# Attention with a gated feed-forward block on one core: probabilities divided by their row sums before the transposes instead of outputs after them, the first pair in written order, the spatial weights split first

## The chip, the cores and the metric

The kernel runs on one core of a Trainium2 chip. The metric is the device time of one execution in microseconds (us); less is better. The time before is the median of three runs. PE is TensorE, DVE is VectorE, ACT is ScalarE, POOL is GpSimd, SP is SyncE, which issues the transfers; PEld is the weight load of TensorE.

## The reference

There are 8 batches, 8 heads, 576 positions and 64 numbers per head. First comes attention with a causal mask in blocks of 64 positions, then one gated feed-forward block over the heads put together (512 columns, 1024 inside), all in float32:

```python
def _attn_ref(q, k, v):
    scores = np.matmul(q, k.transpose(0, 1, 3, 2)) / np.sqrt(64)
    scores = np.where(block_i >= block_j, scores, -1000000000.0)   # blocks of 64
    scores = scores - np.max(scores, axis=-1, keepdims=True)
    attn = np.exp(scores)
    attn = attn / (np.sum(attn, axis=-1, keepdims=True) + 1e-09)
    return np.matmul(attn, v)

def _moe_ref(x, w_in, g_ln, w_sg, b_sg, w_out):       # x: (8, 576, 512)
    h = gelu_tanh(x @ w_in)
    u, v = h[..., :512], h[..., 512:]
    v_n = (v - mu) / np.sqrt(var + 1e-06) * g_ln
    v_s = np.einsum('ts,bsd->btd', w_sg, v_n) + b_sg[None, :, None]
    return x + (u * v_s) @ w_out
```

## The kernel before

**Numbers.** Operands of most matmuls are split into a high and a low part of a TensorE format (`q_h`, `q_l`, `xh`, `xl`, `wi_h`, `wi_l` and so on), and a product is three matmuls: high by high, low by high, high by low. A split is a copy into the high part on VectorE or ScalarE (the rows CAST) and a subtraction on GpSimd. The weights `w_in` and `w_out` come as 64-bit numbers and are put together from their words first (`from_f64`, L199: `Abs` with a scale on ScalarE, three operations on VectorE).

**Attention.** Two heads of one batch make a pair; the 32 pairs are the 32 slots of `slot` (L724). Rows of scores are tiled by five: tile 0 has 64 query rows, tiles 1 to 4 have 128, and tile i needs 64 + 128 i keys (64, 192, 320, 448, 576). For each tile and head, TensorE makes scores (`products`), VectorE adds the mask and finds the negative maximum while it copies them into the tile `prob` (`maximum`, L333, the row CUSTOM_DVE or ISA), and ScalarE takes the exponent in place and leaves the row sums in `sums` (`exponent`, L348). To multiply with `v`, TensorE transposes the probabilities in blocks of 128 columns into PSUM banks `pa`, `pb`, `pc`, `pd` (`turn0`, `turn2`, `turn1`, `turn_first`), ScalarE or VectorE copies the banks out (`pt`), and `av0`, `av2`, `av1` and `av00` add up the output, heads on partitions and positions along the row, in the bank `ob` and a corner of `pd`.

**The row sums.** `inverse` (L438), at the start of a slot, turns all ten sums per row into reciprocals `ri` on VectorE, and GpSimd spreads each over 64 columns (`rx`). `turn_sums` (L456) transposes `rx` in five matmuls into the bank `pe` and a corner of `pd`. `normalise` (L487) copies the output from PSUM to the tile `x` on ScalarE, multiplies it with `pe` and `pd` on VectorE and sends it to a spill buffer in DRAM. `split` (L497) makes `xh` and `xl` of it.

**A slot.** Slot n does the transposes and outputs of pair n and, between them, the scores of pair n + 1, in four steps: the first half of tile 4 and tile 1; the second half of tile 4; tiles 3 and 0; tile 2. Between these stand seven holes, `hole(g[0])` to `hole(g[6])`, each of which takes so many pieces of feed-forward work as the string of the slot says.

**Feed-forward work.** After the fourth pair of a batch, `begin` (L818) queues this batch's parts: five pieces of `v_part`, eight of `u_part`, eight of the batch before's `o_part`, eight of `s_part`. So slots 0 to 3 have no such work, slots 4 to 7 do that of the first batch, and so on; the last batch's stands behind slot 31. `v_part` puts into the queue `side` what other engines do next: the gelu, the moments, the centring and the scaling of the layer norm, which ends in the tiles `vh` and `vl` that `s_part` multiplies with the spatial weights `ws_h`, `ws_l`. `run_side` takes a few of these at set places of a slot. `o_part` (L674) reloads `x` from the spill buffer for the residual (`xr`), one column of 128 at a time, just before its matmuls; `x` and `xr` share a tag of three buffers.

The holes are set by strings, of which the first batch has its own, and the loading of weights by a share for each of the first nine slots:

```python
    WS = [2, 2, 2, 2, 4, 3, 4, 4, 3]
    PLAN = ["1111111", "1111111", "1111111", "1111112"]
    FIRST = ["1111111", "1111111", "1010101", "1010010"]
```

**Weights.** `weights` (L274) is a queue of loading steps: `w_in` for v, the gains `g_ln`, `w_in` for u in two halves, the spatial weights, `w_out`. `load_share(n, k)` takes steps in slot n by `WS`; `need(part)` takes all that are left of a part when the part begins.

**Order.** Only TensorE runs in the order in which the code is written (`PIN = "P"`, L58, L82). What the other engines do in which order, a scheduler decides when the kernel is built. PSUM has five banks for scores, `ob` and feed-forward sums, and three for the transposes, `pd` and `pe`. The first pair's scores are made ahead of slot 0 (L800 to L813), with four loading steps and the split of pair 1 between.

## Time and profile before

| | |
|---|---|
| median of 3 runs | 836.48 us (835.96 to 839.25) |
| profiled execution, its own time | 838.82 us |
| its span | 836.9 us |
| mean granted TensorE clock | 0.966 |
| busy: TensorE, VectorE, ScalarE, GpSimd | 94%, 64%, 51%, 42% |
| weight loads of TensorE, beside its matmuls | 78% |
| the chain that ended last | TensorE 63%, VectorE 20%, ScalarE 6%, transfers 5%, GpSimd 3%, issue 3% |
| DRAM | 45.78 MB read, 18.87 MB written, 77 GB/s over the span |

In the rows of a timeline the first number is the start in us from the span's start, the second the duration, then come engine, line, operation, result <- operands with buffer numbers left out, and the shape; `x4` stands for a run of four such instructions, and the duration is then that of the run. A bracket at the end holds the idle time of the engine just before, and what ended it. In rows of waits the three numbers are the idle time in all, the number of waits, and the longest. Matmuls stand under L86, transposes under L89, and what the other engines do under L99, since helpers record them; so it is the tile's name that tells a step. Two heads' tiles read alike.

Slot 0 begins near 24.4 us, slot 1 at 42.3, slot 2 at 52.9, slot 3 at 64.4, slot 4 at 75.1, slot 8 at 180.7. From there a batch of four slots takes near 97 to 101 us, and the last batch's feed-forward work fills 767.5 to the end.

### The profile page before, as it was taken

Reading aid. Unit: us, or ns where it says so; the run is one execution under the profiler, and the core shown is the slowest. Engines: PE = TensorE matmul, PEld = TensorE weight load, DVE = VectorE, ACT = ScalarE, POOL = GpSimd, SP = SyncE. Lnnn points to the kernel's source line nnn. Section 1 sums busy time; section 2 is a strip of 40 time slices with the busy share of each in tenths; the row PEclk is TensorE's granted clock in tenths of the full one; section 3 lists DMA queues with packets and bytes.
Section 4 is the critical chain, followed back from the end, with each engine's and each line's share of the span. In section 5 each row is a group of like instructions: output and inputs, shape, how many; then the busy total and the mean of one; then the engine's idle time right before and its main releaser. Section 6 shows DMA issues by size and latency. Waiting matters only on the chain.

```text
span 836.9 us, 15898 instructions
## 1 busy us (share of the span) xinstructions
PE 788.5 (94%) x5926; PEld 649.0 (78%) x5926; DVE 531.6 (64%) x1504; ACT 424.4 (51%) x1124; POOL 352.7 (42%) x402
## 2 busy tenths in 40 slices
PE   5798992999999999999999999999999999999998
PEld 3466871878878888887887878788787878878998
DVE  6876474894865658564776747766586647753432
ACT  4776663656654367344653357642764446531400
POOL 5445158461543417432372513634164323713251
PEclk8799995999999999999999999999999999999999
DMA  7233205221122112310133101321123201230031
GB/s 251 77 114 115 85 18 159 80 61 57 44 86 99 58 58 72 126 59 30 58 108 120 58 28 31 126 101 57 58 71 122 77 16 57 75 112 29 1 114 71
DMA packets 46912, 65.67 MB, mean 78 GB/s; under 512 B 4082, under 2 KB 22514, under 8 KB 46836
## 3 DMA queue, kind: packets, MB, share of 16 engines
q1 hardware_dynamic: 46836, 64.67, 24.1%
q8 instruction: 46, 0.75, 0.4%
q14 instruction: 30, 0.25, 0.1%
HBM read 45.78 MB, written 18.87 MB: 77 GB/s over the span
## 4 chain that ended last, share of the span: by engine, by line
PE 63%; DVE 20%; ACT 6%; DMA 5%; POOL 3%; issue 3%; SPq 0%; DVEq 0%; ACTq 0%; POOLq 0%
PE accs L86 14%; PE accv L86 13%; PE acco L86 9%; PE ob L86 9%; PE s L86 7%; PE pb L89 3%; DVE prob L99 3%; DVE bs L99 3%; DVE vh L99 2%; DVE vv L99 2%; PE pa L89 2%; PE accu L86 2%; ACT prob L99 2%; PE pc L89 2%; DMA xr<-spill 2%
## 5 line engine op out<-in xcount | busy, mean ns | idle before, releaser
L99 ACT ACTIVATE prob<-prob,negm 128x448 f32<-128x448 f32 (+3 forms) x320 | 178.0, 558 | 157.8 <-DVE negm L99 154.1
L99 DVE CUSTOM_DVE_ANT_0 prob<-s,mask 128x288 f32<-128x288 f32 (+2 forms) x320 | 119.4, 421 | 37.2 <-PE s L86 36.5
L99 POOL TENSOR_TENSOR q_l<-q_f,q_h 128x576 fp32r<-128x576 f32 x31 | 44.2, 1425 | 196.1 <-PE s L86 158.3
L86 PE MATMUL ob<-pt,v_f 128*64 128x512 f32 (+4 forms) x640 | 115.3, 452 | 0.0
L99 POOL TENSOR_TENSOR gl<-u,gh 128x288 fp32r<-128x288 f32 x64 | 52.3, 824 | 105.1 <-DVE gh L99 72.9
L86 PE MATMUL accs<-ws_h,vh 128*128 128x288 f32 x256 | 79.8, 312 | 8.9 <-DVE vh L99 8.9
L86 PE MATMUL s<-k_h,q_h 64*128 64x288 f32 (+1 forms) x372 | 86.7, 351 | 1.2 <-DVE negm L99 1.2
L86 PE MATMUL accs<-ws_h,vl 128*128 128x288 f32 x256 | 76.8, 300 | 6.1 <-POOL vl L99 6.1
L86 PE MATMUL accu<-xh,wi_h 128*128 128x288 f32 x256 | 78.6, 307 | 1.3 <-ACT wi_h L99 1.3
L86 PE MATMUL acco<-gh,wo_h 128*128 128x288 f32 x256 | 79.8, 312 | 0.0
L86 PE MATMUL acco<-gl,wo_h 128*128 128x288 f32 x256 | 76.5, 299 | 0.0
L86 PE MATMUL acco<-gh,wo_l 128*128 128x288 f32 x256 | 76.4, 299 | 0.0
L86 PE MATMUL accs<-ws_l,vh 128*128 128x288 f32 x256 | 76.2, 298 | 0.0
L86 PE MATMUL accu<-xh,wi_l 128*128 128x288 f32 x256 | 75.4, 295 | 0.3 <-POOL wi_l L99 0.3
L86 PE MATMUL accu<-xl,wi_h 128*128 128x288 f32 x256 | 75.6, 295 | 0.0
L86 PE MATMUL s<-k_l,q_h 64*128 64x288 f32 (+1 forms) x372 | 72.2, 298 | 0.0
L86 PEld LDWEIGHTS ob<-pt,v_f 128*64 128x64 f32 x640 | 40.1, 139 | 40.9 <-issue 20.8
L86 PE MATMUL accv<-wi_h,xh 128*128 128x512 f32 x160 | 66.2, 414 | 0.7 <-POOL xh L99 0.7
L99 DVE TENSOR_TENSOR xr<-acco,xr 128x288 f32<-128x288 f32 x64 | 29.0, 454 | 59.2 <-PE acco L86 21.7
L86 PE MATMUL s<-k_h,q_l 64*128 64x288 f32 (+1 forms) x372 | 66.1, 293 | 0.0
L99 DVE TENSOR_TENSOR u<-accs,u 128x288 f32<-128x288 f32 x64 | 28.7, 448 | 57.6 <-PE accs L86 57.6
L86 PEld LDWEIGHTS s<-k_h,q_h 64*128 64x128 f32 x372 | 49.6, 180 | 18.2 <-issue 12.4
(106 smaller groups left out, 2109.9 us busy)
## 6 DMA issues: line engine op xcount, KB each, us to landing
spill<-x SPq DMA_DIRECT2D x32, 288.0 KB, 3.0
xr<-spill SPq DMA_DIRECT2D x32, 288.0 KB, 3.1
out_T<-xr SPq DMA_DIRECT2D x32, 288.0 KB, 2.4
q_f<-in_qT SPq DMA_DIRECT2D x31, 288.0 KB, 3.1
k_f<-in_kT SPq DMA_DIRECT2D x31, 288.0 KB, 3.4
v_f<-in_v SPq DMA_DIRECT2D x32, 256.0 KB, 3.3
raw<-in_w_in SPq DMA_DIRECT2D x16, 256.0 KB, 5.0
raw<-in_w_out SPq DMA_DIRECT2D x8, 256.0 KB, 4.3
```

The lines of the kernel that those rows point to most:

```text
L86: return pin(nc.tensor.matmul(*a, **k), "P")
L89: return pin(nc.tensor.transpose(out, in_, identity), "P")
L99: return lambda *a, **k: pin(f(*a, **k), self.letter)
```

## The change

**The division moves ahead of the transposes.** `inverse`, `turn_sums` and the two products of `normalise` go; what is left of it, two copies and the spill, is called `leave`. Instead `Scores.divide` stands in three places behind the exponents, for tiles 4 and 1, 3 and 0, and 2: VectorE adds 1e-9 to the sums of those tiles and takes the reciprocals, and each probability tile is multiplied in place with its rows' reciprocals, tiles 4 and 3 on VectorE, 1 and 0 on GpSimd, 2 on ScalarE.

**Order and weights.** For the first pair, VectorE and ScalarE run in written order too, and its loading steps, three now, stand behind it. The spatial weights come second in the queue. `WS` and `FIRST` have other numbers. In `from_f64` the scaling moves from ScalarE to GpSimd.

**Spill and split.** `x` is split at the end of its own slot, except in the first two slots of a batch from the second batch on, whose splits wait until the end of the second one. `o_part` asks for `xr` one column ahead, and for the first column in the next batch's `u_part` (in the last batch, in `s_part`).

```diff
+    kept = set(PIN)
...
-        A.activation(m.bitcast(F32), hi.bitcast(F32), AF.Abs, scale=2.0**-112)
+        G.tensor_scalar(m.bitcast(F32), hi.bitcast(F32), 2.0**-112, None, op0=ALU.mult)
...
             ("v", load_gains()),
+            ("s", load_spatial()),
             ("u0", load_weight(w_in, slice(0, DH // 2), wi_h, wi_l)),
             ("u2", load_weight(w_in, slice(DH // 2, DH), wi_h, wi_l)),
-            ("s", load_spatial()),
...
+        def divide(self, *tiles):
+            i0, i1 = min(tiles), max(tiles)
+            ts = slice(i0, i1 + 1, max(i1 - i0, 1))
+            V.tensor_scalar_add(self.ri[:, ts, :], self.sm[:, ts, :], 1e-9)
+            V.reciprocal(self.ri[:, ts, :], self.ri[:, ts, :])
+            for i in tiles:
+                r, e = slice(0, QN[i]), EXT[i]
+                for a in (0, 1):
+                    x, c = self.prob[a][i][r, :e], self.ri[r, i, a : a + 1]
+                    if i == 2:
+                        A.mul(x, x, c)
+                    else:
+                        {4: V, 3: V, 1: G, 0: G}[i].tensor_scalar(x, x, c, None, op0=ALU.mult)
...
-        def normalise(self):
+        def leave(self):
             x = self.x = page(F32, S, "x")
             copy("a", x[:, BLK:], self.ob)
             copy("a", x[:, :BLK], self.o0)
-            V.tensor_tensor(x[:, BLK:], self.rp, x[:, BLK:], op=ALU.mult)
-            V.tensor_tensor(x[:, :BLK], self.t4[:, 128:192], x[:, :BLK], op=ALU.mult)
...
+        def reload(mo):
+            if mo < NC:
+                x_r[mo] = page(F32, S, "xr")
+                SP.dma_start(x_r[mo], spill.pop((b, mo)))
...
+            if fo == NC - 1 and b:
+                reloads[b - 1](0)
...
             if th == 0:
-                x_r[mo] = page(F32, S, "xr")
-                SP.dma_start(x_r[mo], spill.pop((b, mo)))
+                reload(mo + 1)
...
-    WS = [2, 2, 2, 2, 4, 3, 4, 4, 3]
+    WS = [2, 3, 3, 3, 8, 0, 3, 3, 2]
...
-    FIRST = ["1111111", "1111111", "1010101", "1010010"]
+    FIRST = ["1111111", "1111110", "0000011", "1111110"]
...
-        va.inverse()
         va.turn0(0)
...
             nx.exponents(4)
+            nx.divide(4, 1)
...
             nx.exponents(3, 0)
+            nx.divide(3, 0)
             nx.step4()
         va.av1()
         va.av00()
-        va.turn_sums()
         if nx:
             nx.exponents(2)
+            nx.divide(2)
         hole(g[4])
-        va.normalise()
...
+        va.leave()
+        wait = n // (H // 2) > 0 and n % (H // 2) < 2
+        pending.append(va.split)
+        if not wait:
+            while pending:
+                pending.popleft()()
...
+    kept.update("VA")
     sc = Scores(0)
     sc.step1()
     sc.exponents(1)
     sc.step2()
     sc.exponents(4)
-    weight_step()
+    sc.divide(4, 1)
     sc.step3()
     sc.exponents(3, 0)
-    split_qk(1)
-    weight_step()
+    sc.divide(3, 0)
     sc.step4()
     sc.exponents(2)
-    weight_step()
-    weight_step()
+    sc.divide(2)
+    split_qk(1)
+    for _ in range(3):
+        weight_step()
+    kept.difference_update("VA")
```

Three places show what the change moves. The first is VectorE at the start of the program; the rows ISA with `negm` are the maxima of the first pair, `w<-raw` and `w<-w` are pieces of `w_in`. Before:

```order
1 L99 CAST q_h<-q_f 128x576
2 L99 CAST k_h<-k_f 128x576
3 L99 TENSOR_SCALAR w<-raw 128x256
4 L99 SCALAR_TENSOR_TENSOR w<-raw,w 128x256
5 L99 TENSOR_SCALAR w<-raw 128x256
6 L99 SCALAR_TENSOR_TENSOR w<-w 128x256
7 L99 SCALAR_TENSOR_TENSOR w<-raw,w 128x256
8 L99 TENSOR_SCALAR w<-raw 128x256
9 L99 ISA prob_4_114,negm<-s,mask 128x288
```

After:

```order
9 L101 ISA prob_4_114,negm<-s,mask,negm 128x288
10 L101 ISA negm 128x1
11 L101 ISA prob_4_123,negm<-s,mask,negm 128x288
12 L101 ISA negm 128x1
13 L101 TENSOR_SCALAR ri<-sums 128x2x2
14 L101 RECIPROCAL ri<-ri 128x2x2
15 L101 TENSOR_SCALAR prob_4_114<-prob_4_114,ri 128x576
16 L101 TENSOR_SCALAR prob_4_123<-prob_4_123,ri 128x576
17 L101 ISA prob_3_112,negm<-s,mask 128x448
```

The weight pieces no longer stand ahead of the maxima; instead the division of tile 4, which needs ScalarE's exponents of tiles 4 and 1, stands ahead of the maxima of tile 3.

The second place is VectorE in slot 2, around the maxima of tile 2 of pair 3 (`prob_2_128` and `prob_2_137` are its two heads; `x<-pe,x` is the product with the transposed reciprocals). Before:

```order
L99 CAST q_h<-q_f 128x576
L99 ISA prob_2_128,negm<-s,mask 128x320
L99 ISA negm 128x1
L99 ISA prob_2_137,negm<-s,mask 128x320
L99 ISA negm 128x1
L99 CAST k_h<-k_f 128x576
L99 TENSOR_TENSOR x<-pe,x 128x512
L99 TENSOR_SCALAR ri<-sums 128x10
L99 TENSOR_TENSOR x<-pd,x 128x64
L99 RECIPROCAL ri<-ri 128x10
L99 CAST xh<-x 128x576
```

After:

```order
L101 TENSOR_SCALAR prob_4_132<-prob_4_132,ri 128x576
L101 TENSOR_SCALAR prob_4_141<-prob_4_141,ri 128x576
L101 ISA prob_2_137,negm<-s,mask 128x320
L101 ISA negm 128x1
L101 CAST k_h<-k_f 128x576
L101 TENSOR_SCALAR ri<-sums 128x2x2
L101 CAST xh<-x 128x576
L101 RECIPROCAL ri<-ri 128x2x2
L101 TENSOR_SCALAR ri<-sums 128x2
L101 TENSOR_SCALAR prob_3_130<-prob_3_130,ri 128x448
L101 TENSOR_SCALAR prob_3_139<-prob_3_139,ri 128x448
L101 RECIPROCAL ri<-ri 128x2
```

The products with `pe` and `pd` are gone, and two divisions of tile 3 stand between the sums of tile 2 and their reciprocal.

The third place is ScalarE in slot 9, the second slot of a full batch (`prob_2_110` and `prob_2_119` are tile 2 of the next pair, `u<-u` the gelu of u, ACT_TABLE_LOAD the change of function table). Before:

```order
L99 ACTIVATE prob_2_110,sums<-prob_2_110,negm 128x320
L99 COPY x<-ob 128x512
L99 COPY x<-pd 128x64
L99 ACTIVATE prob_2_119,sums<-prob_2_119,negm 128x320
L99 COPY u<-accu 128x288 x2
L99 ACT_TABLE_LOAD
L99 ACTIVATE u<-u 128x576 x4
L99 COPY pt<-pa 128x512
```

After:

```order
L101 ACTIVATE prob_2_110,sums<-prob_2_110,negm 128x320
L101 COPY x<-ob 128x512
L101 COPY x<-pd 128x64
L101 ACTIVATE prob_2_119,sums<-prob_2_119,negm 128x320
L101 COPY u<-accu 128x288
L101 ACTIVATE prob_2_110<-prob_2_110,ri 128x320
L101 ACTIVATE prob_2_119<-prob_2_119,ri 128x320
L101 COPY u<-accu 128x288
L101 ACT_TABLE_LOAD
L101 ACTIVATE u<-u 128x576 x4
L101 COPY pt<-pa 128x512
```

The two products of the division stand ahead of the last copy of u, the gelu of u and the copy of the bank `pa`.

More of the change, by code (lines that the diff above doesn't have):

```diff
@@ L80, in pbank @@
         return bank("p", name, 3)
+    kept = set(PIN)
     def pin(ins, e):
-        return tc.keep_in_program_order(ins) if e in PIN else ins
+        return tc.keep_in_program_order(ins) if e in kept else ins
     def mm(*a, **k):
@@ L305, in __init__ @@
             self.sm = sp.tile([P, NT, 2], F32, tag="sums", name="sums", bufs=3)
+            self.ri = sp.tile([P, NT, 2], F32, tag="ri", name="ri", bufs=2)
             G.memset(self.sm[:, 0, :], 1.0)
@@ L390, in __init__ @@
             self.v = vals.pop(n)
-            self.prob, self.sm = sc.prob, sc.sm
+            self.prob = sc.prob
             self.pt = {}
@@ L454, in turn_first @@
             copy("a", pt0[:BLK, :], t[:BLK, : 2 * BLK])
-        def turn_sums(self):
-            turn(self.t4[:, 128:256], self.rx[:, 0, :], ident)
-            t = self.rp = pbank("pe")
-            for i in range(1, NT):
-                turn(t[:, (i - 1) * P : i * P], self.rx[:, i, :], ident)
         def av(self, dst, j, pts, c0, n, start, stop):
@@ L522, in paced @@
     def paced(ins, e):
-        return ins if e in PIN else tc.keep_in_program_order(ins)
+        return ins if e in kept else tc.keep_in_program_order(ins)
     def gelu(tiles, after):
@@ L536, in accumulator @@
         return sbank(name)
+    reloads = {}
     def feed_forward(b):
@@ L542, in feed_forward, with v_part @@
         vn_t = sp.tile([P, DH], F32R, tag="vn_t", name="vn_t")
-        parts = (b, vv, vn, vn_t, u, g_s)
+        x_r = {}
+        def reload(mo):
+            if mo < NC:
+                x_r[mo] = page(F32, S, "xr")
+                SP.dma_start(x_r[mo], spill.pop((b, mo)))
+        parts = (b, vv, vn, vn_t, u, g_s, x_r, reload)
         return v_part(*parts), u_part(*parts), s_part(*parts), o_part(*parts)
-    def v_part(b, vv, vn, vn_t, u, g_s):
+    def v_part(b, vv, vn, vn_t, u, g_s, x_r, reload):
         need("v")
@@ L613, in v_part, with u_part @@
             side.append(("V", lambda st=st: scale(st)))
-    def u_part(b, vv, vn, vn_t, u, g_s):
+    def u_part(b, vv, vn, vn_t, u, g_s, x_r, reload):
         x_s = xs.pop(b)
@@ L641, in u_part, with s_part @@
                 yield "u"
-    def s_part(b, vv, vn, vn_t, u, g_s):
+    def s_part(b, vv, vn, vn_t, u, g_s, x_r, reload):
         need("s")
@@ L647, in s_part @@
             run_side(len(side))
+        reloads[b] = reload
         for dt in range(NC):
+            if dt == NC - 1 and b == B - 1:
+                reload(0)
             ghi, glo = page(F32R, S, "gh"), page(F32R, S, "gl")
@@ L672, in s_part, with o_part @@
                 yield "s"
-    def o_part(b, vv, vn, vn_t, u, g_s):
+    def o_part(b, vv, vn, vn_t, u, g_s, x_r, reload):
         need("o")
-        x_r = {}
+        if not x_r:
+            reload(0)
         for mo, th in [(mo, th) for mo in range(NC) for th in (0, 1)]:
@@ L768, in slot @@
         va.av00()
-        va.turn_sums()
         if nx:
             nx.exponents(2)
+            nx.divide(2)
         hole(g[4])
-        va.normalise()
-        last = n % (H // 2) == H // 2 - 1
-        if last:
-            for f in pending:
-                f()
-            pending.clear()
-            va.split()
+        va.leave()
[4 more added lines that the diff above has]
+                pending.popleft()()
         run_side(2)
@@ L788, in slot @@
         run_side(3)
-        for f in pending:
-            f()
-        pending.clear()
-        if not last:
-            pending.append(va.split)
+        if n % (H // 2) == 1:
+            while pending:
+                pending.popleft()()
         return nx
-    pending = []
+    pending = deque()
     last_o = []
```

9 lines of the change are left out of this document (removed).

## The prediction

> **What bounds the kernel now.** I read the page first, for the busy shares and the 40 slices, then a table of stretches cut where a slot begins, then the waits of TensorE, and last the timelines at the places where the table shows TensorE idle.
>
> ```profile
> span 836.9 us, 15898 instructions
> PE   5798992999999999999999999999999999999998
> 24.40:42.30 17.90, 15.27 (x97) 9.21 (x97) 15.66 (x53) 13.27 (x42) 9.61 (x12) 0.75 0.15 47
> 52.90:64.40 11.50, 10.37 (x96) 7.01 (x96) 8.91 (x33) 8.57 (x28) 5.39 (x7) 1.00 0.31 103
> 125.50:146.50 21.00, 6.03 (x24) 4.20 (x23) 8.62 (x9) 7.50 (x12) 18.07 (x18) 0.58 0.51 159
> 479.00:576.00 97.00, 95.89 (x742) 79.59 (x741) 63.99 (x180) 50.89 (x134) 40.71 (x44) 1.00 0.23 74
> ```
>
> In a row of the table the columns are length, TensorE, weight loads, VectorE, ScalarE and GpSimd busy, granted clock, DMA. Three kinds of time show. Four slots of one batch (479 to 576) are filled with matmuls: 95.89 of 97.00. The first slots have attention alone and are nearly full too (10.37 of 11.50), except slot 0, where VectorE has 15.66 of 17.90. And there is a hole of 15 us at 125 to 146, where the granted clock is 0.58. So most of the span goes by what TensorE executes; the opening and the hole go by what it waits for. The hole's waits and owners:
>
> ```profile
> PE accs L86 <- DVE vh L99: 8.9, 3, 5.8
> PE accs L86 <- POOL vl L99: 6.1, 3, 4.7
> 124.90 2.07 SPq L99 DMA_DIRECT2D w<-in_w_sgT  x4
> 134.76 4.63 POOL L99 TENSOR_TENSOR ws_l<-w,ws_h 128x576 fp32r<-128x576 f32 x3
> 136.07 2.06 DVE L99 TENSOR_TENSOR ws_l<-w,ws_l 1x576 fp32r<-1x576 f32 x1 [7.42 <-ACT ws_l L99]
> ```
>
> The spatial matmuls wait 8.9 + 6.1 = 15.0 us for the normalised tiles vh and vl; these stand on VectorE and GpSimd behind the splitting of the spatial weights, whose loads are issued only at 124.90.
>
> **Transposes that go.** Five rx transposes per pair:
>
> ```profile
> 51.56 0.33 PE L89 MATMUL pd<-ident,rx 128*128 128x128 f32 x1
> 52.16 0.38 PE L89 MATMUL pa<-ident,prob 128*128 128x128 f32 x2
> 498.49 0.33 PE L89 MATMUL pd<-ident,rx 128*128 128x128 f32 x1
> 499.01 0.47 PE L86 MATMUL accv<-wi_h,xh 128*128 128x512 f32 x1
> ```
>
> From the first of them to what follows, TensorE spends 0.60 us in the opening and 0.52 in a full slot. From slot 8 on there are 24 pairs, TensorE is full, and nothing else stands in that place: 24 x 0.52 = 12.5 us off (14.4 at 0.60). The pairs before are counted in the next two parts.
>
> **Slots 4 to 7, and the hole.** From the start of slot 4 to that of slot 8:
>
> ```profile
> 75.11 0.38 PE L89 MATMUL pa<-ident,prob 128*128 128x128 f32 x2
> 180.71 0.60 PE L89 MATMUL pa<-ident,prob 128*128 128x128 f32 x4
> 767.51 12.83 PE accv L86 x56
> 780.34 12.74 PE accu L86 x96
> 805.80 14.84 PE accs L86 x112
> ```
>
> That is 105.6 us. The last three rows, from the chain at the end where nothing else runs, price one batch's first three parts: 40.4 us. An attention slot has 10.37 busy less 0.60 for rx, 9.8, four are 39.2; so TensorE needs 79.6. With the spatial weights split in slot 0, what they held up is free. I do not expect 79.6: slot 6 gets no work in its first five holes, so it takes the length of a slot without work (worked out next, 14.8, where its content with two spatial pieces of 1.86 is 13.5: +1.3), the crossing from slot 5 to 6 gets the waits of the part after next (+4.4), and the layer norm still shares GpSimd with the output weights, whose scaling moves there (I allow 4). That makes 89.3, 16.3 off; ends 12 and 20.
>
> **The opening, slots 0 to 3.** Here the division lies open, for no feed-forward work fills the holes.
>
> ```profile
> 5.83 2.37 PE L86 MATMUL s<-w 64*128 64x288 f32 x14
> 12.28 0.45 DVE L99 CUSTOM_DVE_ANT_0 prob<-s,mask 128x288 f32<-128x288 f32 x1
> 24.40 1.56 PE L89 MATMUL pa<-ident,prob 128*128 128x128 f32 x6 [2.66 <-ACT prob L99]
> 50.45 0.46 DVE L99 CAST q_h<-q_f 128x576 fp32r<-128x576 f32 x1 [0.16 <-issue]
> 51.05 1.42 POOL L99 TENSOR_TENSOR q_l<-q_f,q_h 128x576 fp32r<-128x576 f32 x1 [5.35 <-DVE q_h L99]
> 51.65 1.13 DVE L99 CAST k_h<-k_f 128x576 fp32r<-128x576 f32 x1
> 52.65 0.19 ACT L99 ACTIVATION_READ_ACCUMULATOR prob<-prob,negm 128x1 f32 x1
> 52.90 0.44 PE L89 MATMUL pa<-ident,prob 128*128 128x128 f32 x2 [0.36 <-ACT prob L99]
> 53.68 0.20 ACT L99 ACTIVATION_READ_ACCUMULATOR prob<-prob,negm 128x1 f32 x1
> 54.10 0.66 PE L89 MATMUL pa<-ident,prob 128*128 128x128 f32 x4 [0.76 <-DVE x L99]
> 64.38 0.44 PE L89 MATMUL pa<-ident,prob 128*128 128x128 f32 x2 [0.37 <-ACT prob L99]
> ```
>
> The first pair: its maxima now start at 12.28, behind weight pieces. In written order they can start when the first scores are there, near 6.6, a part of the way into the row at 5.83. But VectorE then waits in turn for the exponents of tiles 4 and 1, and of 3 and 0, before the next maxima; adding up its 24 rows with these waits I come to 20.9 for the tile-2 transpose, where 24.40 stood: 3.5 off. Slot 0 then carries eight pieces of w_in, all of the spatial weights and the second pair's divisions through VectorE and GpSimd: between 0 and 9.5 longer than its 17.9 us; I take 5.
>
> Slots 1 to 3 repeat every 64.38 - 52.90 = 11.48 us. Tile 2 closes the loop. Before, head 0's transpose follows its exponent by 0.25 (52.65 to 52.90). Now the reciprocal needs both heads' sums, 1.1 us later (53.68 and its 0.2 stands 1.03 behind the row at 52.65), and on VectorE two more divisions of 128x448 stand between the sums and the reciprocal. Prices: 0.30 each if they run like the cast at 50.45 (0.38 to the next instruction for 576 columns), 0.1 and 0.2 for sum and reciprocal, 0.47 for ScalarE's product of 320 columns, 0.3 for hand-overs: 1.1 + 0.6 + 0.3 + 0.47 + 0.3 = 2.8. Against it 0.76 of wait for x and what hangs on it goes, 1.05 in all, for pe and its products are gone: +1.8 at least.
>
> At most: the cast at 51.65 took 1.13, because GpSimd's q_l ran until 52.47; it ended 0.3 after that. VectorE's divisions are of the same kind (tile in SBUF, no second tensor) and three of them now stand against q_l, k_l and xl, 1.1 + 1.1 + 1.4 = 3.6 more, +5.4. The Trainium skill's page "GPSIMD Engine Reference", section Specifications, says that GpSimd's SBUF interfaces are shared with VectorE, with contention for instructions in a two-port mode; it speaks against this change: by it alone slots 1 to 3 take the upper end, and the sum would be an estimated 831. I take +3.3, between the ends, since not every division will meet a GpSimd instruction. Three slots: +10. The opening in sum: -3.5 + 5 + 10 = +11.5, ends +2 and +22.
>
> **Where a batch is full: slot 1 into 2.** Elsewhere three holes (about 5 us) cover the longer chain. In slot 1 VectorE and GpSimd have the layer norm:
>
> ```profile
> 525.96 1.60 POOL L99 TENSOR_TENSOR k_l<-k_f,k_h 128x576 fp32r<-128x576 f32 x1
> 526.21 1.39 DVE L99 TENSOR_SCALAR ri<-sums 128x10 f32<-128x10 f32 x1
> 526.92 1.03 PE L89 MATMUL pa<-ident,prob 128*128 128x128 f32 x8
> 530.40 2.06 PE L86 MATMUL ob<-pt,v_f 128*64 128x512 f32 x4
> 530.66 0.67 DVE L99 COPY pt<-pa 128x512 f32<-128x512 f32 x1
> 534.39 1.28 POOL L99 TENSOR_TENSOR vl<-vv,vh 128x512 fp32r<-128x512 f32 x1
> 539.44 0.30 PE L89 MATMUL pd<-ident,prob 64*64 64x64 f32 x2 [0.91 <-DVE pt L99]
> L99 DVE TENSOR_TENSOR x<-pe,x 128x512 f32<-128x512 f32 x32 | 21.9, 683 | 3.8 <-PE pa L89 1.7 <-PE pe L89 1.1
> L99 POOL COPY rx<-ri 128x640 f32<-128x640 f32 x32 | 25.9, 811 | 15.7 <-DVE ri L99 15.7
> ```
>
> Even ten numbers (ri) took 1.39 behind GpSimd's k_l. TensorE already loses about 1.0 at 530.40 (2.06, where the pace is 1.08: the copy of 530.66 is late) and 0.91 at 539.44, where VectorE waited for a reload. Off come the products with pe (0.68, with pd's 0.21) and rx on GpSimd (0.81); on go two divisions of 576 and two of 448, two more sums with reciprocals, and four small products on GpSimd, which by rx's 0.81 for 640 columns are some 0.3 each. Three more two-port instructions at 0.35 plus a wait of 1.25 each are 4.8, less 0.9: the last reciprocal comes near 529.5, so tile 2 is turned at 530, not 527, and ScalarE's late product holds the gelu of u and the copy of pa behind it. New waits: 3.6 + 0.8 = 4.4. The earlier reload frees the 0.91: x_r of the next column no longer waits for an out_T to land. Net of the old 1.9 that is +2.5; if the cover holds, -2. Per batch I take +1.0, six times: +6, ends -12 and +18.
>
> **Sum.** +11.5 - 16.3 - 12.5 + 6 = -11.3 on the profiled execution: span 836.9 to 825.6, its own time 838.82 to 827.5. That execution stands 2.3 above the median 836.48; taken from the median it is 825. (About 0.5%, 4 us, is what a measurement of this kernel can tell from none.)
>
> **Rivals.** *VectorE and GpSimd become the bound* (slower). The mechanism is the wait of the row at 526.21. If each division in slots 1 to 3 waits out a GpSimd instruction (+16.2) and slot 0 takes 7.5 more, the opening is +20; the same queue takes 3 from the gain of slots 4 to 7 (-13), and the crossing costs +2.5 a batch (+15). With -12.5 for the transposes that is +9.5: 846. It decides once a slot without work exceeds 15 us and a batch 97. For: in the slot above, GpSimd still has vl at 534.39 of the work begun before 526. Against: over a batch it is busy 40.71 of 97. By the page named above this is the outcome to fear. *The covers hold* (much faster): opening +2, slots 4 to 7 -20, transposes -12.5, crossing -12, in all -42.5 or 794; I say 800, as one of the four will miss. Against it: the chain of slots 1 to 3 cannot be free. *The hole only moves*: the spatial part waits for the layer norm itself, queued behind the output weights and the divisions; 10 of the 15 us come back, 835, no change. For: the rows of vh and vl, not the weights, ended the waits.
>
> **Numbers.** My forecast 0.45, of which 0.40 is over 0.5% faster; covers hold 0.15; VectorE and GpSimd 0.25, of which 0.20 is slower and 0.05 within; the hole moves 0.15 (0.02, 0.10, 0.03). Faster 0.57, same 0.20, slower 0.23. The range leaves out the fast corner and the last of the slow one: 806 to 846; the forecast's own is 815 to 834.
>
> **What would show it.** Right: no wait of accs over 4 us, the tile-2 transpose of the first pair near 21, slots 1 to 3 of 13.3 to 16.9, slot 4 beginning near 87, slot 8 near 176, a batch of about 96. Wrong: slot 4 before 78 (chain hidden) or after 95, or a batch above 98, with TensorE waiting for ScalarE's product of tile 2 in every slot 2.

## The result, and the profile after

The changed kernel takes 905.41 us (median of 4, 905.09 to 906.44); the kernel before takes 836.22 beside it. The ratio is 1.082, with an interval from 1.080 to 1.085: slower by 8%, where 825 was forecast and 846 was the upper end of the range. The head of the page, two of its slices, and four rows of TensorE's waits; the two rows at the end are TensorE's waits in front of `pa` in the kernel before:

```profile
span 903.3 us, 15925 instructions
PE 791.4 (88%) x5766; PEld 649.1 (72%) x5766; DVE 635.6 (70%) x1696; ACT 448.3 (50%) x1164; POOL 448.7 (50%) x522
PE   4655599678997999799997999799997999799998
PEclk7768789688998999899998999899998999999999
PE pa L91 <- ACT prob L101: 57.9, 13, 6.6
PE pa L91 <- DVE prob L101: 30.3, 11, 4.4
...
PE accs L88 <- DVE vh L101: 2.5, 1, 2.5
PE accs L88 <- POOL vl L101: 2.3, 1, 2.3
...
PE pa L89 <- ACT prob L99: 7.7, 5, 4.0
PE pa L89 <- DVE x L99: 2.7, 5, 0.8
```

TensorE is busy about as long as before (791.4 us, before 788.5), but 88 us of waits, where there were 10.4, now stand in front of one tile, `pa`: the first transposes of a pair wait for divided probabilities. The waits for vh and vl, 15.0 us before, are 2.5 and 2.3 now. The slices show the waits twice: in the first third, and as a 7 once per batch. The clock falls with them.

The table of stretches, cut where slot 4 and slot 8 begin, and one batch; the columns are those of the prediction's table:

```profile
0.00:107.08 107.08, 63.30 (x402) 40.52 (x403) 80.82 (x232) 53.44 (x152) 70.50 (x107) 0.73 0.35 111
69.12:87.67 18.55, 11.86 (x93) 7.80 (x91) 13.27 (x50) 11.62 (x36) 8.43 (x11) 0.82 0.21 64
87.67:107.08 19.41, 12.90 (x90) 8.34 (x91) 12.99 (x40) 9.66 (x30) 7.74 (x10) 0.74 0.20 62
107.08:216.96 109.88, 89.94 (x624) 70.78 (x625) 84.06 (x211) 57.33 (x152) 61.49 (x69) 0.88 0.22 68
427.19:529.31 102.12, 95.48 (x723) 79.22 (x722) 75.50 (x204) 54.94 (x143) 49.88 (x56) 0.97 0.22 70
```

The opening has 107.1 us for 75.1 (+32.0), slots 4 to 7 109.9 for 105.6 (+4.3), and what follows 686.3 for 656.2 (+30.1); together +66.4. The product rows of the groups, with count, sum and mean in ns, price what the change added:

```profile
L101 DVE TENSOR_SCALAR prob<-prob,ri 128x448 f32<-128x448 f32 x64 | 66.1, 1073 | 0.5
L101 DVE TENSOR_SCALAR ri<-sums 128x2 f32<-128x2 f32 x32 | 41.9, 1311 | 2.7 <-ACT prob L101 1.9
L101 DVE TENSOR_SCALAR prob<-prob,ri 128x576 f32<-128x576 f32 x64 | 38.4, 642 | 1.0
L101 POOL TENSOR_SCALAR prob<-prob,ri 128x192 f32<-128x192 f32 x64 | 63.1, 995 | 94.8 <-DVE ri L101 92.5 <-ACT wo_h L101 1.6 <-ACT pt L101 0.7
L101 POOL TENSOR_SCALAR prob<-prob,ri 64x64 f32<-64x64 f32 x64 | 34.7, 599 | 39.7 <-DVE ri L101 39.7
```

The row to look at is the second: adding 1e-9 to two numbers per partition takes 1.31 us in the mean. This is where such an addition stands in a batch, at the crossing from its second slot to its third, the timeline of all engines with other rows left out:

```profile
272.04 1.55 POOL L101 TENSOR_TENSOR k_l<-k_f,k_h 128x576 fp32r<-128x576 f32 x1
272.24 1.62 DVE L101 CAST vh<-vv 128x512 fp32r<-128x512 f32 x1
273.56 1.02 POOL L101 TENSOR_SCALAR prob<-prob,ri 64x64 f32<-64x64 f32 x2
273.79 3.04 DVE L101 TENSOR_SCALAR ri<-sums 128x2 f32<-128x2 f32 x1
274.55 1.03 POOL L101 TENSOR_TENSOR vv<-vv,rs 128x512 f32<-128x512 f32 x1
275.55 1.25 POOL L101 TENSOR_TENSOR vl<-vv,vh 128x512 fp32r<-128x512 f32 x1
277.11 0.15 DVE L101 RECIPROCAL ri<-ri 128x2 f32<-128x2 f32 x1
277.36 1.02 ACT L101 ACTIVATE prob<-prob,ri 128x320 f32<-128x320 f32 x2 [6.68 <-DVE ri L101]
277.97 1.54 PE L91 MATMUL pa<-ident,prob 128*128 128x128 f32 x6 [6.56 <-ACT prob L101]
279.80 0.44 PE L88 MATMUL acco<-gh,wo_l 128*128 128x288 f32 x1
```

VectorE's addition begins at 273.79 and ends at 276.83, just behind the last of four GpSimd instructions that follow each other without a gap (two products, vv, vl). The reciprocal, the product on ScalarE and the transposes hang on it: TensorE stands still for 6.56 us. Behind that the matmuls last 0.44, and the stretch 278 to 283 has a granted clock of 0.62, which is, by estimate, 5.00 x 0.38 = 1.9 us more. Such a wait of 6.5 to 6.6 us stands in each of the six batches from slot 8 on (the others end at 379.87, 481.90, 584.03, 686.36 and 789.48), 39.4 us in all. Over the 5 us behind them the granted clock is 0.50 to 0.62; by the same working that is 13.5 us more, so an estimated 53 us.

### The profile page after: what moved, and what is told of

Its sections match the earlier page's. It is cut to its first block, busy times and chain, and to the rows that moved or that the text cites. A ratio compares the mean times of both kernels' runs of the same rounds, so it can differ in the third digit from the quotient of the medians.

```text
span 903.3 us, 15925 instructions
## 1 busy us (share of the span) xinstructions
PE 791.4 (88%) x5766; PEld 649.1 (72%) x5766; DVE 635.6 (70%) x1696; ACT 448.3 (50%) x1164; POOL 448.7 (50%) x522
## 3 DMA queue, kind: packets, MB, share of 16 engines
q1 hardware_dynamic: 46836, 64.67, 22.4%
## 5 line engine op out<-in xcount | busy, mean ns | idle before, releaser
L101 ACT ACTIVATE prob<-prob,negm 128x448 f32<-128x448 f32 (+4 forms) x320 | 177.9, 557 | 166.6 <-DVE negm L101 163.3
L101 POOL TENSOR_SCALAR prob<-prob,ri 64x64 f32<-64x64 f32 (+1 forms) x128 | 97.9, 797 | 134.5 <-DVE ri L101 132.1
L91 PE MATMUL pa<-ident,prob 128*128 128x128 f32 x256 | 48.5, 329 | 88.2 <-ACT prob L101 57.9
L88 PE MATMUL ob<-pt,v_f 128*64 128x512 f32 (+4 forms) x640 | 119.2, 454 | 5.6 <-ACT pt L101 4.9
L101 DVE TENSOR_SCALAR prob<-prob,ri 128x448 f32<-128x448 f32 (+1 forms) x128 | 104.5, 857 | 1.5
L91 PEld LDWEIGHTS pa<-ident,prob 128*128 128x128 f32 x256 | 36.3, 167 | 95.2 <-ACT prob L101 61.8
L101 DVE TENSOR_SCALAR ri<-sums 128x4 f32<-128x4 f32 (+1 forms) x96 | 55.8, 581 | 44.0 <-ACT prob L101 42.9
L88 PE MATMUL acco<-gh,wo_h 128*128 128x288 f32 x256 | 82.2, 321 | 0.0
L88 PE MATMUL acco<-gh,wo_l 128*128 128x288 f32 x256 | 78.8, 308 | 0.0
L101 ACT ACTIVATE prob<-prob,ri 128x320 f32<-128x320 f32 x64 | 32.5, 555 | 90.6 <-DVE ri L101 90.3
```

What stands on the lines that cost most here:

```text
L88: return pin(nc.tensor.matmul(*a, **k), "P")
L91: return pin(nc.tensor.transpose(out, in_, identity), "P")
L101: return lambda *a, **k: pin(f(*a, **k), self.letter)
```

## Experiments

Three theories went into the runs. **Theory 1**: instructions of VectorE that work from and to SBUF (products, casts, additions) wait out GpSimd's instructions, and the division puts many of both on the path. **Theory 2**: the chain sums, reciprocal, product, transpose is long by itself, on whatever engines. **Theory 3**: the new order of weights and tables costs the opening. Each run is read by three stretches of its profiled execution: up to slot 4, slots 4 to 7, and from slot 8 on (us of the span; a stretch ends where the next begins with its first transposes into `pa`). So slots are cut from here on; ahead of the prediction, slots 0 to 3 were cut at their tile-2 transposes. By the first transposes, slots 0 to 3 of the kernel before begin at 16.83, 41.50, 52.16 and 63.63. Every run is built anew, and the scheduler may then order VectorE, ScalarE and GpSimd another way; no run holds that order fixed, so each price below is that of an edit with its new order.

| run | median | to slot 4 | slots 4 to 7 | from slot 8 |
|---|---|---|---|---|
| before | 836.2 | 75.1 | 105.6 | 656.2 |
| after | 905.4 | 107.1 | 109.9 | 686.3 |
| no_division | 805.7 | 84.7 | 93.4 | 625.9 |
| no_add | 864.5 | 105.4 | 104.9 | 652.9 |
| act_10 | 867.2 | 102.9 | 104.3 | 658.6 |
| old_opening | 910.4 | 102.1 | 120.0 | 686.4 |
| act_all_no_add | 843.4 | 101.0 | 100.6 | 640.8 |
| act_10_no_add | 845.4 | 102.4 | 106.3 | 636.1 |
| rest_only | 838.4 | 89.1 | 95.4 | 653.2 |
| before_pool | 849.0 | 77.6 | 105.8 | 663.1 |
| hybrid | 830.9 | 75.6 | 112.1 | 640.6 |
| rest_abs | 831.3 | 85.1 | 93.0 | 650.8 |
| before_spatial | 835.1 | 83.5 | 94.3 | 653.6 |
| before_no_add | 824.2 | 76.8 | 105.2 | 639.8 |
| only_41 | 814.6 | 90.9 | 99.6 | 622.5 |
| busy_wait | 844.1 | 99.6 | 106.4 | 636.0 |
| turned_best | 821.1 | 85.7 | 92.6 | 645.3 |
| hybrid8 | 816.5 | 85.2 | 92.5 | 637.0 |

### What the division costs, and the rest of the change

**no_division.** `divide` returns at once:

```diff
         def divide(self, *tiles):
+            return
```

> The changed kernel without the division: the sums plus 1e-9, the reciprocals and the products with them are left out (the output is then not divided). Everything else of the change stays: no transposed sums, new order of the weights, new tables, first pair in written order. Theory 1 (the division's work on VectorE and GpSimd, which wait for each other, is what costs): slot 4 begins near 75 instead of 107.1, a full batch takes 95 to 97 instead of 102.2, time 800 to 815. Theory 2 (the chain sums, reciprocal, ScalarE's product, transpose is long by itself): also 800 to 815, so this run prices the division and does not part 1 from 2. Theory 3 (the new order of the weights, the tables and the written order of the first pair cost the opening and slots 4 to 7): slot 4 still begins above 95 and the time stays above 835.

805.68 us, ratio 0.962 (0.960 to 0.965). The division costs 99.7 us: 22.4 to slot 4, 16.5 in slots 4 to 7, 60.4 behind. But slot 4 begins at 84.7, not 75: something of the rest costs the opening 10 us, so theory 3 has a part.

**rest_only.** The division goes and the transposed sums come back (`inverse`, `turn_sums` and the two products, as before); all else stays as in the change.

> Everything of the change but the division: transposed sums and the two products with them as before, new order of the weights, new tables, first pair in written order, early reload, new places of the split. Theory 1: the run without any division (805.7) plus 32 pairs of transposes at 0.52, 16.6 us: 820 to 828, so faster than the kernel before. Theory 3 (the new order costs the opening): above 836.

838.40 us, ratio 1.000 (0.999 to 1.002). Theory 1 expected 820 to 828, and the run lies where theory 3 had it, above 836; the miss has two parts. The rest of the change gives 10.2 us in slots 4 to 7 and 3.0 later, and takes 14.0 in the opening. And between this run and no_division there are 33 us, twice the price of the transposes; before_no_add below shows why. The opening's loss is in slot 1:

```profile
35.14:65.97 30.83, 17.46 (x97) 10.48 (x96) 27.73 (x67) 14.93 (x48) 23.39 (x25) 0.67 0.24 73
41.05 1.82 POOL L101 TENSOR_SCALAR w<-raw 128x256 f32<-128x256 f32 x2
42.41 4.03 DVE L101 TENSOR_SCALAR w<-raw 128x256 uint32<-128x256 uint32 x1
42.84 1.39 POOL L101 TENSOR_TENSOR q_l<-q_f,q_h 128x576 fp32r<-128x576 f32 x1
44.20 1.39 POOL L101 TENSOR_TENSOR k_l<-k_f,k_h 128x576 fp32r<-128x576 f32 x1
45.53 0.09 POOL L101 MEMSET sums<- 128x2 f32 x1
45.58 0.71 POOL L101 COPY rx<-ri 128x640 f32<-128x640 f32 x1
```

It lasts 30.8 us, where slot 1 had 10.7 before (41.50 to 52.16), with weight pieces on VectorE and GpSimd. A piece of `w_in` on VectorE takes 4.03 us, to 46.44, and ends just behind GpSimd's row of instructions (two scalings, `q_l`, `k_l`, a memset, `rx`): the same kind of wait as the addition's, with no division in the program.

**old_opening.** Weights, tables, scaling and first pair as before, the division as in the change:

```diff
-            ("s", load_spatial()),
             ("u0", load_weight(w_in, slice(0, DH // 2), wi_h, wi_l)),
             ("u2", load_weight(w_in, slice(DH // 2, DH), wi_h, wi_l)),
+            ("s", load_spatial()),
...
-    FIRST = ["1111111", "1111110", "0000011", "1111110"]
+    FIRST = ["1111111", "1111111", "1010101", "1010010"]
```

> The division, the spill and the split of the change with the weights, the tables, the scaling of the 64-bit words and the order of the first pair as before. Theory 1: slots 0 to 3 and the crossings still wait: a batch stays near 102.2; slot 4 begins at 98 to 108, slots 4 to 7 take 108 to 118; time 895 to 915. Theory 3: the batches stay, but the first 217 us shrink by 20 or more; time 875 to 885.

910.35 us, ratio 1.086 (1.084 to 1.088), as theory 1 expected, but for slots 4 to 7, which take 120.0 and not up to 118. The new order is worth 5 us beside the division; theory 3 does not explain the loss.

**before_spatial** and **rest_abs.** The kernel before with the new order of weights and the new `WS` and `FIRST` alone; and rest_only with the scaling back on ScalarE:

```diff
-        G.tensor_scalar(m.bitcast(F32), hi.bitcast(F32), 2.0**-112, None, op0=ALU.mult)
+        A.activation(m.bitcast(F32), hi.bitcast(F32), AF.Abs, scale=2.0**-112)
```

> The kernel before with the new order of the weights and the new tables alone. By the rest_only run the hole gives about 10 us and the opening takes it back, so 833 to 840 if the spatial weights cost the opening; if it was the written order of the first pair or the scaling on GpSimd that cost it, slot 4 begins near 78 and the time is 822 to 830.

> rest_only (838.4: all of the change but the division) with the scaling of the 64-bit words on ScalarE, as before. Theory 1: GpSimd loses 24 instructions of 1.0 us, 16 of them in the first 90 us, and VectorE's pieces of w_in wait less: slot 4 begins at 80 to 85 instead of 89.1, time 829 to 835. Theory 3 in its narrow form (it is the spatial weights, split in slots 0 and 1, that cost the opening, whoever scales): slot 4 at 87 to 90, time 836 to 840.

835.12 us, ratio 0.997 (0.995 to 0.999), and 831.28, ratio 0.992 (0.990 to 0.994). The weights' order gives 11.3 in slots 4 to 7 and takes 8.4 in the opening; the scaling on GpSimd was another 4.0 of the opening, which theory 1 had expected. That the weights' order costs the opening by the same waits between the engines is not shown.

### The waits between VectorE and GpSimd

**no_add.** The addition of 1e-9 is left out:

```diff
-            V.tensor_scalar_add(self.ri[:, ts, :], self.sm[:, ts, :], 1e-9)
-            V.reciprocal(self.ri[:, ts, :], self.ri[:, ts, :])
+            V.reciprocal(self.ri[:, ts, :], self.sm[:, ts, :])
```

> The changed kernel with the reciprocals taken straight from the sums: the addition of 1e-9 on VectorE is left out (every sum is at least 1, where float32 has no room for it). One VectorE instruction of 2 or 4 columns less in each of three places per pair. Theory 1 (VectorE's products, casts and additions wait out the GpSimd instruction that runs, a reciprocal does not): the 3.04 us of the addition at 273.79 go, the wait of 6.56 in front of tile 2 at the crossing from the second slot to the third falls to about 3.5, a batch to near 98, the opening by 1.2 in each of three slots; time 872 to 888. Theory 2 (length of the chain by itself): an addition of 2 columns is worth 0.1 us; 898 to 905. Theory 3 (weights and tables): 898 to 905.

864.52 us, ratio 1.032 (1.029 to 1.034): 40.9 us for three instructions of 2 or 4 columns a pair, more than either theory had. A batch falls from 102.1 to 97.1. The place of the wait moves on; the crossing of a later batch in this run:

```profile
452.90 0.99 POOL L101 TENSOR_SCALAR prob<-prob,ri 64x64 f32<-64x64 f32 x2
453.50 3.06 DVE L101 CAST k_h<-k_f 128x576 fp32r<-128x576 f32 x1
453.86 1.03 POOL L101 TENSOR_TENSOR vv<-vv,rs 128x512 f32<-128x512 f32 x1
454.86 1.39 POOL L101 TENSOR_TENSOR q_l<-q_f,q_h 128x576 fp32r<-128x576 f32 x1
457.62 0.69 PE L91 MATMUL pa<-ident,prob 128*128 128x128 f32 x2 [3.36 <-ACT prob L101]
L101 DVE CAST k_h<-k_f 128x576 fp32r<-128x576 f32 x31 | 46.1, 1486 | 0.0
```

Now the cast of k lasts 3.06 us, through GpSimd's row, and its mean is 1486 ns where the change has 929. The transposes still wait 3.36, half of 6.56. GpSimd's order has changed too (`vv` and `q_l` behind the products, not `vv` and `vl`), so not all of the 40.9 need be the addition's own.

**act_10** and **act_10_no_add.** The small products go to ScalarE, alone and with no_add:

```diff
-                    if i == 2:
+                    if i < 3:
                         A.mul(x, x, c)
```

> The changed kernel with the products of tiles 1 and 0 on ScalarE instead of GpSimd; GpSimd has 97.9 us less to do, ScalarE about 50 more. Theory 1: in the crossing two 0.5 us products of GpSimd go from its queue (q_l, k_l, prob, vv, vl), the addition's wait ends 1.0 earlier, and 2.0 of the 3 us a slot of the opening loses goes; a batch near 100.5, slot 4 near 98, time 882 to 895. Theory 2: two more products of 0.46 and 0.33 a head on ScalarE ahead of tile 2 make the chain longer, time 905 to 915. Theory 3: 903 to 908.

> Both single edits together: tiles 1 and 0 on ScalarE, no addition of 1e-9; VectorE keeps the four products of tiles 4 and 3. Alone they gave 864.5 and 867.2 from 905.4. Theory 1: they take away two parts of the same wait, so not the whole sum of 79; time 838 to 855, a batch 95.5 to 97, slot 4 begins near 98 to 102. Theory 2: no better than 864.5.

867.16 us, ratio 1.035 (1.033 to 1.038), and 845.38, ratio 1.009 (1.006 to 1.011). Taking 98 us off GpSimd gains 38.2 us, with more of ScalarE's products on the chain: against theory 2. The addition of two columns is still there in act_10, but takes 0.65 us in the mean and 1.36 at most, where the change has 1.31 and 3.04. Together the two edits give 60.0 of the single sums of 79, as expected of two parts of one wait. From slot 8 on there is nothing left of the loss:

```profile
208.67:844.80 636.13, 616.95 (x4742) 522.42 (x4740) 417.14 (x1178) 367.13 (x949) 249.34 (x255) 1.00 0.23 73
```

The clock is 1.00 there, and a batch takes 94.66.

**act_all_no_add.** All ten products on ScalarE:

```diff
-                    if i == 2:
-                        A.mul(x, x, c)
-                    else:
-                        {4: V, 3: V, 1: G, 0: G}[i].tensor_scalar(x, x, c, None, op0=ALU.mult)
+                    A.mul(x, x, c)
```

> The changed kernel with all ten products of a pair on ScalarE and the reciprocals straight from the sums (the addition of 1e-9 is left out): no instruction of the division is left on VectorE and GpSimd that waits for the other engine. By the exponents' durations (0.77, 0.66, 0.56, 0.46, 0.33) ScalarE's share rises by 4.4 us a pair to about 73 of 97 us a batch. Theory 1 (VectorE and GpSimd wait for each other): slots 1 to 3 take 13 to 15 instead of 18.5 to 20.5, no wait at the crossing above 2, a batch 95 to 97, time 825 to 848. Theory 2 (the chain by itself): four more products stand ahead of tile 2's on ScalarE, the crossing waits 4 or more, time 860 to 885.

843.42 us, ratio 1.006 (1.004 to 1.009), within theory 1's range. But slots 2 and 3 take 17.2 and 15.9, not 13 to 15, and slot 4 begins at 101: in the opening, theory 1 is not all.

**before_pool.** The other way round, four GpSimd products with factor 1.0 added to the kernel before:

```diff
+        def idle_products(self, i):
+            r, e = slice(0, QN[i]), EXT[i]
+            for a in (0, 1):
+                x = self.prob[a][i][r, :e]
+                G.tensor_scalar(x, x, 1.0, None, op0=ALU.mult)
```

> The kernel before with GpSimd's four products per pair of the change, in place on tiles 1 and 0 with the factor 1.0 behind their exponents; nothing else of the change, so the output is the same. GpSimd gets about 98 us more work. Theory 1: VectorE's casts and the addition of ten sums wait out more GpSimd instructions: slots 1 to 3 take 12.5 to 15 instead of 11.5, a batch 97.5 to 100, time 845 to 865. Theory 2: no VectorE or ScalarE step is added to the chain of tile 2, GpSimd was busy for 42% only; 836 to 842.

849.03 us, ratio 1.014 (1.010 to 1.017). GpSimd's work alone costs 11 us, 1.5 a batch, with no division in the program, and TensorE's waits have no row for these products themselves; the total is as expected, though slots 2 and 3 (12.2 each) came out a little below.

**before_no_add.** The kernel before with `V.reciprocal` straight from the ten sums:

```diff
-            V.tensor_scalar_add(r, self.sm.rearrange("p i a -> p (i a)"), 1e-9)
-            V.reciprocal(r, r)
+            V.reciprocal(r, self.sm.rearrange("p i a -> p (i a)"))
```

> The kernel before with the reciprocals straight from the ten sums, without the addition of 1e-9, which took 1.0 us in the middle case there. Theory 1: the wait is the same as in the change, but nobody on the path to TensorE waits for it (GpSimd spreads the reciprocals, the transposes come at the slot's end); 833 to 838, no change that counts. If it were the number of waits and not their place that decides: 27 us of VectorE less, time 815 to 828.

824.17 us, ratio 0.984 (0.982 to 0.986). My expectation failed: I had held that nobody on the path waits for this addition, and the time lies in the other range, 815 to 828. What waits is what is queued behind it on VectorE, the copy of `pa` and the copies that the transposes into `pd` need:

```profile
PE pd L89 <- DVE pt L99: 1.2, 3, 0.5
424.30 0.68 DVE L99 COPY pt<-pa 128x512 f32<-128x512 f32 x1
373.43:468.76 95.33, 94.91 (x743) 79.40 (x741) 61.22 (x175) 50.91 (x134) 40.45 (x44) 1.00 0.24 76
```

The copy comes 2.73 us behind its transposes at 421.57, where it came 3.74 behind in the prediction's rows (526.92 and 530.66); the waits into `pd` fall from 6.9 to 1.2 in all; a batch takes 95.3. From slot 8 on the addition was worth 16.4 us. Of the 27.3 between rest_only and no_division in that stretch that leaves about 10.9 for the transposes, if the addition costs the same in both kernels. Without that condition: full batches take 95.2 to 95.6 in before_no_add and 95.3 to 95.6 in turned_best, against 93.2 in no_division, so 2.0 to 2.4 a batch or 12 to 15 in six, for the transposes with their two products and reciprocals. Both lie near the 12.5 of the prediction.

### The opening, the clock, and what the division is worth

**only_41.** act_10_no_add with `divide(3, 0)` and `divide(2)` left out:

```diff
             nx.exponents(3, 0)
-            nx.divide(3, 0)
...
             nx.exponents(2)
-            nx.divide(2)
```

> act_10_no_add (845.4) with the division of tiles 3, 0 and 2 left out: only tiles 4 and 1 are divided (the output is then only partly divided), so nothing of the division stands behind the last two steps of scores. In the opening, act_10_no_add still loses 5.7 us in each of slots 2 and 3 against the run without division. Theory 2, now for the opening alone (the chain behind the last scores is long by itself): slots 1 to 3 fall from 17.3 and 16.9 to 11.2 to 12.0, slot 4 begins at 86 to 91 instead of 102.4, time 808 to 818. Theory 1 alone (it is still the two engines' waiting): the products of tile 4 and the casts wait as before, slots 2 and 3 stay above 14, slot 4 above 95, time above 830.

814.56 us, ratio 0.973 (0.968 to 0.978). Slot 4 begins at 90.9 instead of 102.4: as theory 2 expected for the opening. There 11.5 us hang on the divisions behind the last two steps of scores, where no feed-forward piece fills the holes. The edit takes tile 3's products off VectorE too, so by itself it does not part the chain from the engines' waiting; act_all_no_add does, which has no product on VectorE or GpSimd and kept slots 2 and 3 at 17.2 and 15.9. So the 22.4 us that the division costs to slot 4 fall into 4.7 that act_10_no_add gets back, these 11.5, and 6.2 for tiles 4 and 1. Slot 2 falls from 17.3 to 11.2 and slot 3 from 16.9 to 13.6, above what was expected; slot 1 takes 26.6, with the weight pieces.

**busy_wait.** act_10_no_add with idle transposes in TensorE's wait:

```diff
             for i in (4, 3, 2, 1):
+                if i == 3 and a == 0 and 0 < self.n < 4:
+                    for _ in range(24):
+                        turn(t[:, 2 * P : 3 * P], ident, ident)
                 self.turn(a, t[:, (i - 1) * P : i * P], i, 0)
```

> act_10_no_add (845.4) with 24 idle transposes of the identity ahead of tile 3's first transpose in slots 1 to 3, where TensorE waits 3.8 us: they are overwritten at once, and the output is the same. If the lower clock comes from TensorE's idling, the granted clock of slots 2 and 3 rises from 0.80 to 0.95 or more and each is shorter by the 1.5 to 2.2 us that its matmuls now take longer (12.4 busy instead of 10.0 to 10.4): time 839 to 842. If the clock does not follow from idling, the idle transposes change nothing or cost up to 1 us a slot: 845 to 849.

844.11 us, ratio 1.009 (1.006 to 1.011): between its two expectations, and in the whole not to be told from act_10_no_add. The slots tell more. First slots 2 and 3 of act_10_no_add, then of this run:

```profile
68.24:85.53 17.29, 12.26 (x94) 7.87 (x90) 11.49 (x38) 10.99 (x34) 4.54 (x5) 0.80 0.22 70
85.53:102.39 16.86, 12.48 (x94) 8.08 (x91) 10.88 (x37) 10.85 (x34) 5.05 (x5) 0.80 0.23 71
```

```profile
67.80:85.18 17.38, 14.02 (x119) 9.80 (x115) 12.30 (x37) 11.43 (x36) 7.32 (x8) 0.90 0.24 69
85.18:99.55 14.37, 12.45 (x119) 9.09 (x115) 10.90 (x37) 10.86 (x34) 5.06 (x5) 1.00 0.27 83
```

Where the idle transposes held the clock at 1.00 (slot 3), the slot is 2.5 us shorter, and the other engines held it up no less: tile 3's first transpose comes 4.10 us and tile 2's 5.19 us behind the slot's start in both runs, and all of the gain lies behind that. In slot 2 the clock came to 0.90 and nothing was gained: there more pieces of `w_in` stand on GpSimd than in act_10_no_add (7.32 us busy against 4.54), and tile 2's transposes come 6.64 us behind the slot's start where they came 5.84, which takes back the 0.7 us gained behind them. So the clock follows from idling, and its price is 2.5 us in the one slot that shows it alone.

**hybrid.** The division from pair 4 on (with the two edits of act_10_no_add), the opening as before; **turned_best**, rest_abs without the addition; **hybrid8**, turned_best up to pair 7 and the division from pair 8 on:

```diff
         def divide(self, *tiles):
+            if self.n < TURNED:
+                return
...
+        if n < TURNED:
+            va.inverse()
...
+        if n < TURNED:
+            va.turn_sums()
```

> The division ahead of the transposes from the fifth pair on only, where feed-forward work covers its chain, with tiles 1 and 0 on ScalarE and the reciprocals straight from the sums; the first four pairs keep the transposed sums; weights, tables and first pair as before, reload and split as in the change. Theory 1: the opening and slots 4 to 7 cost what they did before (75.1 and 105.6), the rest what act_10_no_add needs from slot 8 on (636.1): a span of 817, time 812 to 824, faster than both kernels. Theory 2 (the chain by itself): slots 4 to 7 lie as open as the opening did, time 828 to 840.

> The rest of the change with the transposed sums, the scaling on ScalarE (rest_abs, 831.3) and the ten reciprocals straight from the sums, which took 14.2 off the kernel before: a batch of 95.2, time 814 to 820. If the addition's wait was another one than the crossing's, which the change's early reload has partly taken off already: 822 to 829.

> turned_best for the first eight pairs, then the division ahead of the transposes with tiles 1 and 0 on ScalarE and no addition: slot 8 begins near 177, and then act_10_no_add's 636.1: time 812 to 818. Against turned_best the division gains 0.5 us a batch (94.66 against 95.17), so within 5 us of it; if the division still loses where it begins (slot 7 and 8), slower than turned_best.

830.86 us, ratio 0.991 (0.990 to 0.993); 821.07, ratio 0.981 (0.977 to 0.986); 816.53, ratio 0.976 (0.972 to 0.979). hybrid kept the old opening (75.6) as expected, but lost 6.5 in slots 4 to 7 and came out where theory 2 had it (828 to 840): TensorE waits 3.05 and 1.06 us for divided tiles where slot 4 begins and 1.87 where slot 7 does. turned_best scattered from 817.3 to 825.4 (the table's row is the highest of these) and came out between its two expectations. hybrid8 beats both kernels, by 2.4% and 9.8%. Against turned_best its median is 4.5 us lower, but the two ratios' intervals overlap; in the traces its full batches take 94.66 against 95.25 to 95.57. So the division ahead of the transposes is worth 0.6 to 0.9 us a batch here, with its additions and small products out of the two engines' way, and whether it gains more than that is not shown.

## Why the prediction was wrong

The sum failed in three places: the opening was forecast at +11.5 and came to +32.0, slots 4 to 7 at -16.3 and came to +4.3, and the rest at -6.5 (-12.5 and +6) and came to +30.1.

**The first pair: right.** The tile-2 transposes were forecast at 20.9; they stand at 19.85.

**Weights in slots 0 and 1: wrong.** The step took -3.5 and +5, 1.5 us for the new order. Without any division the opening is 14.0 us longer (rest_only), 4.0 of it by the scaling on GpSimd. I looked at slot 0 alone; in that run slot 1 was the one that grew, by 20 us. In the change itself, cut at the first transposes, slot 0 is 12.5 us longer than before and slot 1 9.9, where +5 and +3.3 stood.

**Slots 1 to 3: the terms were too small, and one was missing.** The step took +3.3 a slot, at most +5.4. Measured are 18.55 and 19.41 for slots 2 and 3 against 11.48, so +7.1 and +7.9. The four GpSimd products were put at 0.3 us each (in the part on slot 1 into 2) by the copy into rx; they take 1.0 and 0.6. TensorE's own work in such a slot takes 11.9 to 12.9 us instead of 10.4 at a clock of 0.74 to 0.82: idling lowers the clock, and the sum had no term for it. The chain behind the last scores, which I priced at 2.8 less 1.05 a slot, is worth 6.1 and 3.3 in slots 2 and 3 of only_41, the lower clock in it.

**Slots 4 to 7: right in the cause, wrong in what came in its place.** Forecast was 16.3 less. The spatial weights' early split gives 10.2 to 12.6 (rest_only, rest_abs). With the division the four slots are 4.3 longer than before, since slots 4 and 6 begin with waits for tiles 3 and 2 as slots 1 to 3 do: 4.29 and 1.76 us in slot 4, for which no term stood, and 4.40 and 3.31 in slot 6, for which 4.4 stood. Against rest_only slot 4 is 6.5 us longer and slot 6 8.0, which is all of the difference between the two runs there.

**The transposes: right in size.** 12.5 was forecast; the runs leave about 11 to 15 for them and what hangs on them.

**The crossing: this step failed worst.** It read "three more two-port instructions at 0.35 plus a wait of 1.25 each", and took +1.0 us a batch; its upper end of +18 is 3.0 a batch, though the working stops at 2.5. The place, the mechanism and the row (the addition at 526.21) were right. The bound was not: I let VectorE wait for one GpSimd instruction, since 1.25 to 1.6 is what one takes, and it can wait out a row of them. The longest GpSimd instruction takes 1.75 us in the change, where the addition took 3.04; 1.76 in no_add, where the cast of k took 3.06; and 2.63 in rest_only, where a piece of `w_in` took 4.03. So what stood at 4.4 us of new waits a batch at the most came out as one of 6.56 with an estimated 1.9 to 2.5 for the clock behind it. Over six batches that is the estimated 53 us; less the old 1.9 a batch and 12 for the transposes it comes to 30, as measured. That is a sum that fits, not a measurement of its own. The last row is act_10's:

```profile
L101 POOL TENSOR_TENSOR k_l<-k_f,k_h x31: 1418/1546/1624, 22.5 to 783.5; 128x576 fp32r<-128x576 f32 x31
L101 DVE TENSOR_SCALAR ri<-sums x96: 152/170/3043, 10.4 to 808.0; 128x4 f32<-128x4 f32 x64, 128x2 f32<-128x2 f32 x32
L101 DVE RECIPROCAL ri<-ri x96: 146/169/182, 10.6 to 808.2; 128x4 f32<-128x4 f32 x64, 128x2 f32<-128x2 f32 x32
L101 DVE TENSOR_SCALAR ri<-sums x96: 152/170/1357, 10.6 to 770.6; 128x4 f32<-128x4 f32 x64, 128x2 f32<-128x2 f32 x32
```

In these rows stand the shortest, the middle and the longest duration in ns. In the change the addition ranges from 152 to 3043; the reciprocal of the same numbers on the same engine never waits (146 to 182), nor does it in no_add, where it stands in the addition's place (147 to 184). The Trainium skill's page "SBUF — State Buffer", in the section on who interferes with whom, says that VectorE's `copy`, `cast` and `tensor_scalar` can run in a mode that takes ports shared with GpSimd, and that the second to come then blocks until the first has finished. The trace agrees in that additions, products and casts are what waits, and goes beyond it: the wait can span several GpSimd instructions. Why VectorE gets in at some boundaries between two of them (before, at 527.6) and not at others, no run here tells. What the traces do tell is where it happens: VectorE instructions of over 1.9 us stand 57 times in the four runs whose GpSimd has the small products (19 after, 13 in no_add, 18 in old_opening, 7 in before_pool), and five times in the other fourteen together (one before, two each in rest_only and hybrid).

**The rivals.** "VectorE and GpSimd become the bound" had the mechanism, and its conditions (a slot above 15 us, a batch above 97) both came true; its price of 846 was 60 too low for the reasons above. "The hole only moves" did not come true: TensorE's waits for vh and vl fell from 15.0 us to 4.8, and what stands in slot 6 now is a wait for divided tiles. Under "wrong" the prediction named the signs itself, and all came: slot 4 after 95, a batch above 98, and TensorE waiting for ScalarE's product of tile 2 in each crossing.

## What to carry to other kernels

Before work is put on VectorE and GpSimd at once, ask which VectorE instructions can be held up by GpSimd, and put the upper end of the price of each at the length of GpSimd's whole row of ready instructions, not at one of them; the smallest instruction on the path, here an addition of two columns, can be the dearest. What stands in the queue behind it waits too, even where its own result is not urgent. And a wait of several us costs TensorE more than its length, since the granted clock is lower behind it (here 0.50 to 0.62 over the 5 us behind waits of 6.5).

## What the runs showed of the hardware

- A VectorE addition of two columns took from 0.15 to 3.04 us, a reciprocal of the same columns 0.15 to 0.17, in one execution.
- GpSimd's product of 128x192 with one number per row took 1.0 us and of 64x64 0.6, VectorE's of 128x576 and 128x448 0.64 and 1.07 in the mean. At best these took 0.51 and 0.43, so the larger mean of the shorter tile is waiting.
- Behind a TensorE wait of 6.56 us the granted clock was 0.62 over the next 5 us; with waits of 5.0 and 4.4 us in two slots it was 0.80 over each, and in the second of them 1.00 where idle transposes took up most of one wait.
